# A decode-attention kernel without the GpSimd library: the identity and the maximum over partitions made by other engines

## The chip, the cores and the metric

The kernel runs on one core of one Trainium2 chip. The metric is the device time of one execution in microseconds (us); lower is better. The kernel before took 439.23 us, the median of its first three runs (438.93 to 439.62). One-core runs of one kernel agree within about 0.3%.

Names used below: PE is TensorE, PEld its weight loads, DVE VectorE, ACT ScalarE, POOL GpSimd, SP SyncE, which issues the loads. `L338` is line 338 of the kernel that the profile belongs to, so the same operation has another line in each kernel. "KB" in the lists of issues is 1024 bytes.

## The reference, cut to what matters

```python
def _A_ref(x, k_cache, v_cache, wq, wo):         # B=4, D=512, 32 query heads, 8 kv heads, Sk=8192, Dh=128
    q = (x @ wq) ...                             # one query token per batch
    scores = einsum("bhqd,bhkd->bhqk", q, k) * Dh ** -0.5
    p = softmax(scores, axis=-1)
    o = einsum("bhqk,bhkd->bhqd", p, v)
    return o @ wo
# _B_ref: the same with only the last W = 2048 positions of its cache
return concatenate([a, b], axis=-1)
```

Both caches are read once, in bf16. With the weights that is 184.56 MB, and almost no arithmetic per byte.

## The kernel before

The work is cut into 20 units, four for B and then 16 for A. Each unit has 4 MB of K and 4 MB of V. Two units make one turn of a hardware loop. A unit's K is transposed on PE in 16 steps, evicted by DVE and ACT in turn, and multiplied with the queries. Then the softmax follows: maximum along the free axis on DVE, maximum over the partitions on POOL, subtraction on DVE, exponential on ACT. PV, the product with V, runs on PE one unit later. The parts that the change touches:

```python
def pool_ar1(u):                                    # the maximum over partitions, a library operation
    n = ncol(u)
    def fn(pool):
        return pool.partition_all_reduce(MB[:, 0:n], M1m[:, 0:n], channels=128, reduce_op=ReduceOp.max)
    return dict(eng="pool", fn=fn, waits=[("pm", u, 0)], inc=("ar1", u))

def pool_setup0(pool):                              # all memsets first
    ...                                             # dummy, onesf, onesb, RQ, OT_sb, oacc, PT
    return pool.memset(Wo_sb[:, :, :], 0.0)
op("pool", pool_setup0, inc=("pset",))
def pool_setup1(pool):                              # then the identity, bf16 and fp32
    ins = pool.affine_select(out=ident[:, :], in_=onesb[:, :], pattern=[[1, 128]], compare_op=AluOpType.is_equal, ...)
    ins = pool.affine_select(out=identf[:, :], in_=onesf[:, :], ...)
    return ins
op("pool", pool_setup1, waits=[("pset",)], inc=("setup",))
...
# the order of PE in a unit: T0 T1 T2 (T3 S0) ... T15 S12, sums of u-1, S13, X, S14, S15, PV0 ... PV7 of u-1
# the order of DVE after the last scores:
add(dve_max(u, 1)); ...; add(dve_addmask(u))
add(dve_sum(u - 1)); add(dve_rcp(u - 1))            # beside the all-reduce
add(dve_submask(u)); add(dve_sub(u, 0)); add(dve_sub(u, 1)); add_norm(u - 1)
```

PE waits on absolute semaphore counts, so each turn ends by taking the turn's share off every semaphore that PE waits on:

```python
with nc.Fori(0, n_turn, engines=[engine]):
    run(turns[0])
    for n, sem in by_name.items():
        pe.sem_inc(sem, -strides[n])
```

The loads are issued by SP in one queue: Wq of B, Wq of A, K of unit 0, K of unit 1, then V and K of the following units as their two buffer slots come free, and at the end the last quarter of Wo in eight pieces (`Wl_sb`).

## Time and profile before

| what | number | how to read it |
|---|---|---|
| time, span of the profile | 439.23 us, 437.0 us | the span is the profiled execution |
| DMA, queue q1 | 99.1% of 16 engines | the loads fill the span |
| PE busy | 365.0 us, 84% | second |
| DVE, ACT, POOL busy | 48%, 45%, 6% | far from full |
| last weight piece lands | about 434.4 us | PE's last waits are for it |

The profile's other lines of before are shown in the prediction below. L888 is the line with the `sem_inc` above; "PEq" is PE's sequencer:

```profile
PE KT L283 <- PEq L888: 4.1, 3, 1.4
```

PE's first transposes of a turn stand up to 1.4 us behind those resets. In the trace's records of PE's sequencer the last loop end of before has 11 resets, from 425.08 to 426.59 us, 0.15 us apart.

### The profile page before, as it was taken

Reading aid. Unit: us, or ns where it says so; the run is one execution under the profiler, and the core shown is the slowest. Engines: PE = TensorE matmul, PEld = TensorE weight load, DVE = VectorE, ACT = ScalarE, POOL = GpSimd, SP = SyncE. Lnnn points to the kernel's source line nnn. Section 1 sums busy time; section 2 is a strip of 40 time slices with the busy share of each in tenths; the row PEclk is TensorE's granted clock in tenths of the full one; section 3 lists DMA queues with packets and bytes.
Section 4 is the critical chain, followed back from the end, with each engine's and each line's share of the span. In section 5 each row is a group of like instructions: output and inputs, shape, how many; then the busy total and the mean of one; then the engine's idle time right before and its main releaser. Section 6 shows DMA issues by size and latency. Waiting matters only on the chain.

```text
span 437.0 us, 15525 instructions
## 1 busy us (share of the span) xinstructions
PE 365.0 (84%) x7174; PEld 337.9 (77%) x7184; DVE 210.0 (48%) x406; ACT 195.0 (45%) x249; POOL 27.7 (6%) x88
## 2 busy tenths in 40 slices
PE   0168898998998959895989598969868996989996
PEld 0158897997997949795979588868868886979975
DVE  0004455664564634563456247525643563455651
ACT  1024473573653625371634254434534462536530
POOL 6100000000000000000000000000100000000000
PEclk9999999999999988999999899989996999799999
DMA  8999999999999999999999999999999999999996
GB/s 340 430 421 421 429 412 430 418 439 412 445 432 432 424 438 432 432 432 432 432 432 429 432 432 430 431 433 432 410 454 432 432 432 432 432 432 411 447 407 255
DMA packets 10996, 184.73 MB, mean 423 GB/s; under 512 B 1236, under 2 KB 2280, under 8 KB 2408
## 3 DMA queue, kind: packets, MB, share of 16 engines
q1 hardware_dynamic: 10960, 184.56, 99.1%
q8 instruction: 8, 0.13, 0.1%
q14 instruction: 4, 0.03, 0.0%
q10 hardware_dynamic: 24, 0.01, 0.0%
HBM read 184.56 MB, written 0.01 MB: 422 GB/s over the span
## 4 chain that ended last, share of the span: by engine, by line
PE 54%; DMA 40%; issue 2%; DVE 1%; SPq 1%; ACT 1%
DMA K_sb<-in_A_k_cache_dram 29%; PE KT L283 27%; PE OT L338 11%; DMA K_sb<-in_B_k_cache_dram 7%; PE SB L322 5%; PE SA L322 4%; DMA V_sb<-in_A_v_cache_dram 4%; PE KT L396 4%; PE SA L350 1%; PE KT L338 1%; SPq L566 1%; DVE oacc L404 1%; PE KT L263 1%; ACT KT_sb L299 1%; DVE OS L501 0%
## 5 line engine op out<-in xcount | busy, mean ns | idle before, releaser
L283 PE MATMUL KT<-identf,K_sb 128*128 128x128 f32 x1280 | 207.6, 296 | 44.1 <-DMA K_sb<-in_A_k_cache_dram 30.7
L299 ACT ACTIVATE KT_sb<-KT 128x1024 bf16<-128x1024 bf16 (+1 forms) x192 | 165.1, 881 | 120.6 <-PE KT L283 120.6
L283 PEld LDWEIGHTS KT<-identf,K_sb 128*128 128x128 f32 x1280 | 147.6, 150 | 49.3 <-DMA K_sb<-in_A_k_cache_dram 31.7
L299 DVE COPY KT_sb<-KT 128x512 int32<-128x512 int32 x160 | 110.5, 691 | 132.1 <-PE KT L283 130.7
L338 PE MATMUL OT<-PT,V_sb 128*128 128x64 bf16 x2560 | 78.1, 193 | 1.6 <-issue 1.1
L338 PEld LDWEIGHTS OT<-PT,V_sb 128*128 128x128 bf16 x2560 | 75.9, 98 | 1.8 <-issue 1.2
L469 ACT ACTIVATE PT<-Dt 128x512 bf16<-128x512 f32 x40 | 24.6, 630 | 84.0 <-DVE Dt L458 84.0
L322 PEld LDWEIGHTS SA<-RQc,KT_sb 128*128 128x128 bf16 x1280 | 56.9, 98 | 2.3
L322 PEld LDWEIGHTS SB<-RQc,KT_sb 128*128 128x128 bf16 x1280 | 51.1, 97 | 7.9 <-issue 4.4
L322 PE MATMUL SA<-RQc,KT_sb 128*128 128x16 bf16 x1280 | 56.4, 170 | 0.0
L322 PE MATMUL SB<-RQc,KT_sb 128*128 128x16 bf16 x1280 | 52.9, 170 | 0.0
L420 DVE TENSOR_REDUCE M<-SB 128x8 f32<-128x512 f32 (+1 forms) x20 | 13.8, 692 | 50.0 <-PE SB L322 50.0
L441 POOL PARTITION_ALL_REDUCE MB<-M1m x20 | 7.7, 387 | 334.3 <-DVE M1m L434 334.3
L396 PE MATMUL KT<-Wo_sb,OL 128*4 128x512 bf16 x80 | 18.9, 379 | 0.0
L201 PE MATMUL KT<-ident,x_sb 4*128 4x4 bf16 x8 | 0.6, 170 | 19.9 <-POOL identf L537 19.9
L201 PEld LDWEIGHTS KT<-ident,x_sb 4*128 4x128 bf16 x8 | 0.4, 112 | 20.1 <-issue 20.1
L476 DVE TENSOR_REDUCE LB<-SA 128x8 f32<-128x512 f32 (+1 forms) x20 | 13.7, 684 | 2.8 <-PE SA L350 2.8
L458 DVE TENSOR_TENSOR Dt<-SA,MBm 128x512 f32<-128x512 f32 x20 | 13.8, 692 | 0.7
L367 DVE TENSOR_TENSOR ORx<-KT,MSK 32x1024 bf16<-32x1024 bf16 x10 | 12.1, 1211 | 3.3 <-PE KT L362 3.3
L458 DVE TENSOR_TENSOR Dt<-SB,MBm 128x512 f32<-128x512 f32 x20 | 13.6, 681 | 0.0
L420 DVE TENSOR_REDUCE M<-SA 128x8 f32<-128x512 f32 (+1 forms) x20 | 13.6, 681 | 0.0
L350 PE MATMUL SA<-PT,onesb 128*128 128x128 bf16 x168 | 12.7, 218 | 0.0
(69 smaller groups left out, 118.0 us busy)
## 6 DMA issues: line engine op xcount, KB each, us to landing
K_sb<-in_A_k_cache_dram SPq DMA_DIRECT2D x15, 4096.0 KB, 22.5
V_sb<-in_A_v_cache_dram SPq DMA_DIRECT2D x15, 4096.0 KB, 30.3
K_sb<-in_B_k_cache_dram SPq DMA_DIRECT2D x8, 2048.0 KB, 23.6
V_sb<-in_B_v_cache_dram SPq DMA_DIRECT2D x16, 1024.0 KB, 18.4
V_sb<-in_B_wq_dram SPq DMA_DIRECT2D x1, 4096.0 KB, 12.5
V_sb<-in_A_wq_dram SPq DMA_DIRECT2D x1, 4096.0 KB, 21.8
Wo_sb<-in_B_wo_dram SPq DMA_DIRECT2D x4, 1024.0 KB, 11.9
K_sb<-in_A_k_cache_dram SPq DMA_DIRECT2D x2, 2048.0 KB, 17.5
```

Source lines behind the costliest of these rows:

```text
L283: ins = pe.transpose(out=bkf[:, pi * 128:(pi + 1) * 128], in_=K_sbf[:, slot, t0:t0 + 2, :].rearrange("p t d -> p (t d)"), identity=identf[ ...
L299: ins = e.tensor_copy(out=d, in_=r) if eng == "dve" else e.activation(out=d, in_=r, func=ACTF.Copy)
L322: ins = pe.matmul(out=stb[:, t % NTH * C:(t % NTH + 2) * C], lhsT=ktv[:, pi, :, e], rhs=RQc[:, u % 2, t // TS, e, :], start=(e == 0), stop ...
L338: ins = pe.matmul(out=otb[:, s * NW:s * NW + w], lhsT=V_sb[:, slot, t, :], rhs=PT[:, slot, t * C:t * C + w], start=(j == 0), stop=(j == n ...
L350: ins = pe.matmul(out=SA[u % 2][:, s * NM:(s + 1) * NM], lhsT=onesb[:, :], rhs=PT[:, u % 2, c0:c0 + NM], start=(i == 0), stop=(i == n - 1))
L367: return dve.tensor_tensor(out=ORx[:, :, :, :], in0=bk[0:NR, 0:128].rearrange("p (i o r) -> p r o i", o=1, r=C).broadcast_to([NR, C, C, 12 ...
L396: ins = pe.matmul(out=bk[0:Bn, 0:D], lhsT=OL[:, i, :], rhs=Wo_sb[:, i, :], start=(i == 0), stop=(i == C - 1))
L420: return dve.tensor_reduce(out=M1[:, h * n:(h + 1) * n].rearrange("p (s h) -> p s h", h=C), in_=bank[:, :].rearrange("p (s j h) -> p s h j ...
L441: return pool.partition_all_reduce(MB[:, 0:n], M1m[:, 0:n], channels=128, reduce_op=ReduceOp.max)
L458: return dve.tensor_tensor(out=Dt[:, h * NTH * C:(h + 1) * NTH * C].rearrange("p (s j h) -> p s j h", s=Sh, h=C), in0=bank[:, :].rearrange ...
L469: return act.activation(out=PT[:, u % 2, a:b], in_=Dt[:, a:b], func=ACTF.Exp, scale=scale)
L476: return dve.tensor_reduce(out=LB[:, 0:n].rearrange("p (s h) -> p s h", h=C), in_=SA[u % 2][:, 0:NSEG * NM].rearrange("p (s j h) -> p s h ...
```

## The change

The intent is to do without the GpSimd library, whose load was taken to hold up the start (the gap of 11.13 us in the prediction's lines). The identity comes from a running sum on VectorE, a 32x32 transpose and a comparison, copied to four diagonal blocks; the long memsets go behind it. The maximum over partitions becomes a PE transpose, a VectorE maximum, a diagonal matrix, and a PE product with ones that spreads it to all partitions. Core of the diff (cuts marked):

```diff
-                return pool.partition_all_reduce(MB[:, 0:n], M1m[:, 0:n], channels=128, reduce_op=ReduceOp.max)
+        def pe_MT(u):
+            op("pe", lambda pe: pe.transpose(out=mtx(u), in_=M1m[:, :], identity=identf[:, :]), waits=[("pm", u, 0)], inc=("mt", u))
+        def dve_mx(u):     # tensor_reduce max of mtx(u) into MX, waits mt
+        def dve_dg(u):     # DG = identf * MX (a diagonal), waits mx
+        def pe_MB(u):
+            op("pe", lambda pe: pe.matmul(out=mbx(u), lhsT=onesf[0:NX, :], rhs=DG[:, :], start=True, stop=True), waits=[("dg", u)], inc=("ar1", u))
...
-        def pool_setup1(pool):
-            ins = pool.affine_select(out=ident[:, :], ...
+        op("pool", lambda pool: pool.memset(ONE[:, :], 1.0), inc=("pl", 0))
+        op("dve", lambda dve: dve.tensor_tensor_scan(out=JC, data0=ONE, data1=ONE, initial=0.0, op0=mult, op1=add), ...)
+        op("dve", lambda dve: dve.transpose(out=JR, in_=JC), ...)
+        op("dve", lambda dve: dve.tensor_tensor(out=EQ, in0=JC, in1=JR, op=is_equal), ...)
+        def pool_identf(pool):    # EQ to the four diagonal 32x32 blocks of identf; ident is a copy of identf
...
+        op("pool", pool_setup, inc=("pset",))       # the memsets, now after the masks
...
+            if pc == 3: TOK.append(("MT",))         # PE: transpose after three PV chunks
+            if pc == 5: TOK.append(("MB",))         # PE: broadcast after five
...
+            if u >= 1:
+                add(dve_sum(u - 1))                 # the sum moves ahead of the second maximum
             add(dve_max(u, 1))
```

Left out of the cut: GpSimd's copies of the queries wait for a new signal from PE (`rqf`), and PE, DVE and ACT wait for the moved memsets (`pset`).

More of the change, by code (lines that the diff above doesn't have):

```diff
@@ L28, in bass_concat_heads__gqa_block_cached__sliding_block_cached__decode_kernel @@
 ):
-    ReduceOp = bass.bass_isa.ReduceOp
     Bn, _, D = A_x.shape
@@ L99, in bass_concat_heads__gqa_block_cached__sliding_block_cached__decode_kernel @@
         M1m = sb("M1m", [128, NSEG * C], F32)
-        MB = sb("MB", [128, NSEG * C], F32)
         MBm = sb("MBm", [128, NSEG * C], F32)
@@ L114, in bass_concat_heads__gqa_block_cached__sliding_block_cached__decode_kernel @@
         ORx = sb("ORx", [C * Bn, C, C, 128 // C], BF16)
+        ONE = sb("ONE", [128, 32], F32)
+        JC = sb("JC", [128, 32], F32)
+        JR = sb("JR", [128, 32], F32)
+        EQ = sb("EQ", [128, 32], F32)
+        MX = sb("MX", [NSEG * C, 1], F32)
+        DG = sb("DG", [NSEG * C, NSEG * C], F32)
         MSK = sb("MSK", [C * Bn, C], BF16)
@@ L128, in bass_concat_heads__gqa_block_cached__sliding_block_cached__decode_kernel @@
                  "out0", "out1", "out2", "Tq", "Td", "Ta", "S", "PV", "Ed", "Ea", "Eq", "vs", "sub", "exp", "otr", "otp",
-                 "ocp", "Ef", "fin0", "fin1", "ar1", "SM", "msk", "pset", "setup", "pm0", "pm1", "oc", "ocB", "mkb", "perm", "rq"]
+                 "ocp", "Ef", "fin0", "fin1", "ar1", "mt", "rqf", "dg", "jj", "pl", "SM", "msk", "pset", "setup", "pm0", "pm1", "oc", "ocB", "mkb", "perm", "rq"]
         sems = {n: sm("s_" + n) for n in names}
@@ L159, in sem_of @@
                 return sems["Ed"] if jobs[key[1]]["eng"] == "dve" else sems["Ea"]
-            return sems["vs" if t in ("max", "maxc", "sum", "rcp", "os") else t]
+            return sems["vs" if t in ("max", "maxc", "sum", "rcp", "os", "mx") else t]
         DMA_KEYS = ("K", "Kh", "KH", "V", "Vh", "VL", "WL", "x", "out", "WQ", "wo")
@@ L253, in efn @@
                 return ins
-            add(dict(eng="act", fn=efn, waits=[("T", idx)], inc=("E", idx)))
+            add(dict(eng="act", fn=efn, waits=[("T", idx), ("pset",)], inc=("E", idx)))
         def pe_filler(n):
@@ L304, in pool_rq @@
             un = units[u]
-            w = [("E", perm_idx[un["P"]])]
+            w = [("E", perm_idx[un["P"]])] + ([("rqf", u - 2)] if u >= 2 else [])
             if un["P"] == 1:
@@ L340, in fn @@
                 return ins
-            op("pe", fn, waits=waits, inc=("PV", u * NC + c))
+            op("pe", fn, waits=waits, inc=("rqf", u + 1) if c == 0 and bank is None else ("PV", u * NC + c))
         def pe_SM(u):
@@ L435, in dve_addmask, with mtx, mbx @@
             return dict(eng="dve", fn=fn, waits=[("max", u, 1) if P == 1 else ("maxc", u)] + ([("mkb",)] if u == 0 else []), inc=("pm", u, 0))
-        def pool_ar1(u):
-            n = ncol(u)
-            def fn(pool):
-                return pool.partition_all_reduce(MB[:, 0:n], M1m[:, 0:n], channels=128, reduce_op=ReduceOp.max)
-            return dict(eng="pool", fn=fn, waits=[("pm", u, 0)], inc=("ar1", u))
+        NX = NSEG * C
+        def mtx(u):
+            return SA[(u + 1) % 2][0:NX, 0:128]
+        def mbx(u):
+            return SA[(u + 1) % 2][:, 128:128 + NX]
+        def pe_MT(u):
+            op("pe", lambda pe: pe.transpose(out=mtx(u), in_=M1m[:, :], identity=identf[:, :]), waits=[("pm", u, 0)], inc=("mt", u))
+        def dve_mx(u):
+            n = ncol(u)
+            return dict(eng="dve", fn=lambda dve: dve.tensor_reduce(out=MX[0:n, :], in_=mtx(u)[0:n, :], axis=AX.X, op=AluOpType.max),
+                        waits=[("mt", u)], inc=("mx", u))
+        def dve_dg(u):
+            n = ncol(u)
+            return dict(eng="dve", fn=lambda dve: dve.tensor_scalar(out=DG[0:n, :], in0=identf[0:n, 0:NX], scalar1=MX[0:n, :], scalar2=None,
+                                                                    op0=AluOpType.mult), waits=[("mx", u)], inc=("dg", u))
+        def pe_MB(u):
+            op("pe", lambda pe: pe.matmul(out=mbx(u), lhsT=onesf[0:NX, :], rhs=DG[:, :], start=True, stop=True), waits=[("dg", u)], inc=("ar1", u))
         def dve_submask(u):
@@ L447, in fn @@
             def fn(dve):
-                return dve.tensor_tensor(out=MBm[:, 0:n], in0=MB[:, 0:n], in1=MASK[P][:, 0:n], op=AluOpType.subtract)
+                return dve.tensor_tensor(out=MBm[:, 0:n], in0=mbx(u)[:, 0:n], in1=MASK[P][:, 0:n], op=AluOpType.subtract)
             return dict(eng="dve", fn=fn, waits=[("ar1", u)], inc=("pm", u, 1))
@@ L520, in pool_otp, with pool_first @@
             return dict(eng="pool", fn=lambda pool: pool.tensor_copy(out=OTp[:, :, :], in_=OT_sb[:, P, q, :, :]), waits=w, inc=("otp", tn))
-        def pool_setup0(pool):
+        def pool_first(pool):
+            pool.memset(identf[:, :], 0.0)
             pool.memset(dummy[:, :], 0.0)
             pool.memset(onesf[:, :], 1.0)
-            pool.memset(onesb[:, :], 1.0)
-            pool.memset(RQ[0][:, :, :, :, :], 0.0)
-            pool.memset(RQ[1][:, :, :, :, :], 0.0)
-            pool.memset(OT_sb[:, :, :, :, :], 0.0)
-            pool.memset(oacc[:, :], 0.0)
-            pool.memset(PT[:, :, :], 0.0)
-            return pool.memset(Wo_sb[:, :, :], 0.0)
-        op("pool", pool_setup0, inc=("pset",))
-        def pool_setup1(pool):
-            ins = pool.affine_select(out=ident[:, :], in_=onesb[:, :], pattern=[[1, 128]],
-                                     compare_op=AluOpType.is_equal, fill=0.0, base=0, channel_multiplier=-1)
-            ins = pool.affine_select(out=identf[:, :], in_=onesf[:, :], pattern=[[1, 128]],
-                                     compare_op=AluOpType.is_equal, fill=0.0, base=0, channel_multiplier=-1)
-            return ins
-        op("pool", pool_setup1, waits=[("pset",)], inc=("setup",))
+            return pool.memset(onesb[:, :], 1.0)
+        op("pool", lambda pool: pool.memset(ONE[:, :], 1.0), inc=("pl", 0))
+        op("pool", pool_first, inc=("pl", 1))
+        op("dve", lambda dve: dve.tensor_tensor_scan(out=JC[:, :], data0=ONE[:, :], data1=ONE[:, :], initial=0.0, op0=AluOpType.mult,
+                                                     op1=AluOpType.add), waits=[("pl", 0)], inc=("jj", 0))
+        op("dve", lambda dve: dve.transpose(out=JR[:, :], in_=JC[:, :]), waits=[("jj", 0)], inc=("jj", 1))
+        op("dve", lambda dve: dve.tensor_tensor(out=EQ[:, :], in0=JC[:, :], in1=JR[:, :], op=AluOpType.is_equal), waits=[("jj", 1)], inc=("jj", 2))
+        def pool_identf(pool):
+            ins = None
+            for q in range(4):
+                ins = pool.tensor_copy(out=identf[32 * q:32 * q + 32, 32 * q:32 * q + 32], in_=EQ[32 * q:32 * q + 32, :])
+            return ins
+        op("pool", pool_identf, waits=[("jj", 2), ("pl", 1)], inc=("pl", 2))
+        op("pool", lambda pool: pool.tensor_copy(out=ident[:, :], in_=identf[:, :]), waits=[("pl", 2)], inc=("setup",))
         def pool_perm(pool):
@@ L562, in bass_concat_heads__gqa_block_cached__sliding_block_cached__decode_kernel, with pool_setup @@
         op("pool", pool_mask2, waits=[("msk",)], inc=("mkb",))
+        def pool_setup(pool):
+            pool.memset(RQ[1][:, :, :, :, :], 0.0)
+            pool.memset(RQ[0][:, :, :, :, :], 0.0)
+            pool.memset(OT_sb[:, :, :, :, :], 0.0)
+            pool.memset(oacc[:, :], 0.0)
+            pool.memset(PT[:, :, :], 0.0)
+            return pool.memset(Wo_sb[:, :, :], 0.0)
+        op("pool", pool_setup, inc=("pset",))
         def dma(dst, src):
@@ L579, in bass_concat_heads__gqa_block_cached__sliding_block_cached__decode_kernel @@
             pe_job_perm(P)
-        op("pe", None, waits=[("E", perm_idx[0]), ("setup",), ("msk",)])
-        op("dve", None, waits=[("msk",)])
+        op("pe", None, waits=[("E", perm_idx[0]), ("setup",), ("msk",), ("pset",)])
+        op("dve", None, waits=[("msk",), ("pset",)])
         add(pool_rq(0))
@@ L598, in bass_concat_heads__gqa_block_cached__sliding_block_cached__decode_kernel @@
             pc += 1
+            if pc == 3:
+                TOK.append(("MT",))
+            if pc == 5:
+                TOK.append(("MB",))
         assert pc == NC
@@ L624, in bass_concat_heads__gqa_block_cached__sliding_block_cached__decode_kernel @@
                     pe_SM(u - 1)
+                elif tok[0] == "MT":
+                    pe_MT(u)
+                elif tok[0] == "MB":
+                    pe_MB(u)
                 else:
@@ L643, in bass_concat_heads__gqa_block_cached__sliding_block_cached__decode_kernel @@
             if u >= 1:
-                add(dve_sum(u - 1))
                 add(dve_rcp(u - 1))
+            add(dve_mx(u))
+            add(dve_dg(u))
             add(dve_submask(u))
@@ L667, in bass_concat_heads__gqa_block_cached__sliding_block_cached__decode_kernel @@
                 add(pool_rq(u + 1))
-            add(pool_ar1(u))
             if u >= 1 and units[u - 1]["P"] == 0:
```

## The prediction

> **What bounds the kernel now.** I read the page from the top: busy shares, the tenths by slice, the DMA queue table.
>
> ```profile
> span 437.0 us, 15525 instructions
> DMA  8999999999999999999999999999999999999996
> GB/s 340 430 421 421 429 412 430 418 439 412 445 432 432 424 438 432 432 432 432 432 432 429 432 432 430 431 433 432 410 454 432 432 432 432 432 432 411 447 407 255
> q1 hardware_dynamic: 10960, 184.56, 99.1%
> ```
>
> The 16 DMA engines are full in every slice but the first and the last, and move 432 GB/s in most. 184.56 MB at 432 GB/s is 427.2 us, which leaves 9.8 us of the 437.0 us span for the start, a slightly slower first third, and the tail. PE, at 84% busy, is second. The question for this change is therefore not what an engine saves, but whether the DMA queue starts earlier, runs dry, or is followed by a longer tail.
>
> Second, the windows view over stretches I chose. Columns: window, length, busy time of PE, PEld, DVE, ACT, POOL with counts, PE clock, DMA share, GB/s.
>
> ```profile
> 8.00:19.20 11.20, 0.00 (x0) 0.00 (x0) 0.00 (x0) 0.00 (x0) 0.12 (x1) 1.00 0.99 424
> 34.00:90.00 56.00, 53.24 (x1027) 50.03 (x1030) 30.77 (x54) 29.82 (x55) 2.24 (x7) 1.00 1.01 422
> 141.00:270.00 129.00, 109.21 (x2066) 101.55 (x2070) 65.15 (x126) 58.49 (x62) 5.92 (x24) 0.95 1.00 431
> ```
>
> From 8 to 19 us every compute engine is idle while DMA runs at 99%. From 34 to 90 us PE is nearly full as well (53.24 of 56): it is catching up. From 141 us on it has 15% to spare.
>
> Third, the chain that ended last, in order of time (start, length, what):
>
> ```profile
> 2.38 31.46 DMA K_sb<-in_B_k_cache_dram
> 33.88 3.68 PE KT L283 x16
> ...
> 408.76 17.94 DMA V_sb<-in_A_v_cache_dram
> ```
>
> The first cache block lands at 33.84 us because it stands behind two 4 MB Wq loads in one queue. Nothing on the compute side touches that. The last V load is waited for too.
>
> Fourth, the timeline of the start (start, length, engine, line, operation) with the queue's issues:
>
> ```profile
> 4.62 3.51 POOL L531 MEMSET Wo_sb<- 128x4096 bf16 x1
> 19.26 0.28 POOL L535 TENSOR_SCALAR_AFFINE_SELECT ident<-onesb 128x128 bf16<-128x128 bf16 x1 [11.13 <-issue]
> 24.15 2.94 SPq L566 DMA_DIRECT2D V_sb<-in_B_v_cache_dram  x4
> ```
>
> The memsets end at 8.13 us, then GpSimd stands 11.13 us before the first select: the library load that the change removes. The identity exists at 19.8 us, the first V loads are issued at 24.15 us.
>
> Fifth, the timeline of one unit's end (unit 18), where the reduction sits:
>
> ```profile
> 404.41 3.89 PE L338 MATMUL OT<-PT,V_sb 128*128 128x64 bf16 x128
> ...
> 405.51 0.17 DVE L434 TENSOR_TENSOR M1m<-M1c,MASKA 128x8 f32<-128x8 f32 x1
> 405.60 0.68 DVE L476 TENSOR_REDUCE LB<-SA 128x8 f32<-128x512 f32 x1
> 405.78 0.37 POOL L441 PARTITION_ALL_REDUCE MB<-M1m  x1 [13.96 <-DVE M1m L434]
> 406.32 0.20 DVE L483 RECIPROCAL RL<-LB 128x8 f32<-128x8 f32 x1
> 406.44 0.11 DVE L448 TENSOR_TENSOR MBm<-MB,MASKA 128x8 f32<-128x8 f32 x1
> ...
> 407.19 0.68 DVE L458 TENSOR_TENSOR Dt<-SB,MBm 128x512 f32<-128x512 f32 x1
> ```
>
> The all-reduce takes 0.37 us and hides wholly behind VectorE's sum and reciprocal: VectorE goes from one to the next without a gap. It is not slow once loaded.
>
> **What the Trainium skill says.** "DMA: Bandwidth & Descriptors", section "Where 436 GB/s comes from", gives 435.2 GB/s as the fabric ceiling, but says that for HBM to SBUF about 358 binds. The trace has 431 GB/s for 129 us, so here the fabric ceiling is the one that fits, and there is no rate left to win. "GPSIMD Engine Reference", section "When to use GPSIMD", lists the cross-partition reduce as GpSimd's alone; in the trace it costs 387 ns on average; I found no page with the 11 us load. "VectorE: DVE Perf Modes", section "The TRN2 errata", gives (N+151)/0.96 ns for an fp32 two-input operation: 691 for 512 elements against 692 in the trace, and 166 for 8 elements against 167. I use it for the new small operations. "TensorE: Matmul & The Clock Gate", section "PE-mode transpose", gives about 275 ns in a kernel for a 128x128 bf16 transpose; the trace's fp32 ones on L283 take 296 ns each and four of them advance PE by 0.49 us.
>
> **The change part by part.** (1) Start. Removed: 11.13 us of library load and the 8 us of memsets ahead of the identity, which move behind it. Added: some ten small operations on VectorE and GpSimd at 0.1 to 0.3 us (rows of that size take that), with a few hand-overs: the identity should be there at about 3 us instead of 19.8. The moved memsets are then done at about 11 us. But the first Q projection needs Wq for B, whose load was issued at 0.80 us and lands at about 13.3 us (12.5 us median landing in the table of DMA issues), so it starts at about 13.5 us instead of 20.5, and the first V loads are issued at about 17 us instead of 24.15. At 24.15 us the queue had 16 MiB (16.8 MB) issued and, by the GB/s row, 9.4 MB moved: 17 us of work. An earlier issue only lengthens it. Worth on the end: 0 us. Wq for A lands at about 23 us and K at 33.84 us as before, so PE starts the caches at the same 33.9 us.
>
> (2) Per unit, 20 times. GpSimd loses 0.37 us, nobody's bound. The sum moves ahead of the second maximum, into VectorE's 1.87 us wait for the last scores: free. PE gets an fp32 transpose after three of the eight PV chunks and an fp32 matmul after five. A chunk is 3.75/8 = 0.47 us, so PE reaches the transpose at 404.41 + 1.41 = 405.82 us, and the masked maxima are ready at 405.68: no wait, or a tenth. The transpose costs PE about 0.15 to 0.2 us of issue; its result is there at about 406.15. Maximum over 128: (128+151)/0.96 = 0.29 us; diagonal: 0.17 us; ready at about 406.7. PE comes to the broadcast at 405.82 + 0.2 + 0.94 = 406.96, so again does not wait; an fp32 product is two passes in this trace (L679), say 0.3 us of issue, result at about 407.3. The subtraction of the mask starts there instead of at 406.44: 0.9 us later. Both subtractions end at about 408.8 (before 407.87). PE's last chunk ends 0.2 + 0.3 = 0.5 us later, so the norm and the next unit's first eviction shift by 0.5 us. Sum: 0.5 us per unit on PE and VectorE, 10 us in all, of which the question is how much shows.
>
> (3) Does the queue run dry? Taking issued megabytes from the list of issues and moved ones from the GB/s row: at 54.77 us 25.2 MB issued and 22.4 moved, 2.8 MB or 6.5 us in hand; at 123.99 us 54.5 and 51.9, 6.1 us in hand; at 183.97 us 80.7 and 77.8, 6.9 us in hand. Up to 124 us PE never waits for K, so delays add up: five units, 2.5 us, against 6.1. After that each pair of units starts with a K landing (30.7 us of such waits, in 8 turns), which forgives the delay of the pair before: 1 us against 6.9. The queue stays full: 0 us.
>
> (4) Tail. The last wait for K before the end is at 370.7 us; four units follow, 2.0 us of delay, of which the 0.5 us wait for V at 421.85 and the 1.3 us wait at 427.08 take 1.8.
>
> ```profile
> 427.08 1.98 PE L338 MATMUL KT<-PT,V_sb 128*128 128x64 bf16 x64 [1.33 <-DMA V_sb<-in_A_v_cache_dram]
> ...
> 434.47 0.08 PEld L700 LDWEIGHTS KT<-Wl_sb,OT_sb 128*4 128x4 bf16 x1 [0.23 <-DMA Wl_sb<-in_A_wo_dram]
> ```
>
> What is left, 0.2 us, meets a 0.46 us wait for V at 430.4 and small waits for Wl. Worth 0 to 0.3 us. Sum: 439.23 + 0 + 0 + 0.1 = 439.3 us.
>
> **Rivals.** (a) The start is on the path and its 11 to 17 us are won: about 425 us. For it: PE sat 19.9 us before its first instruction, its longest single wait. Against: the DMA share of 0.99 in those microseconds, and a floor of 427.2 us at this rate before any tail. (b) PE meets VectorE in order and stalls twice a unit, 1 us or more each: 20 units by 2 us or more empty the 6 us cushion before 124 us, and the tail grows: 442 to 455 us. For it: PE at 53.24 of 56 us and my slacks of 0.14 and 0.26 us are thin. Against: one missed slack costs tenths, not a microsecond. (c) The library load takes memory traffic that the packet table does not list: 0.3 to 0.7 us won. The rate of 424 while it loads, against 431 later, leaves room for 0.2 us at most; a start at 394 from 2 to 8 us is before it. (d) Each unit's delay is 1 us instead of 0.5: the tail gets 1 to 2 us, 440 to 441 us.
>
> **Range and chances.** The three runs before span 0.7 us; (c) pulls down by half a microsecond, (d) up by one. 438.5 to 440.4 us. Faster by 2% needs 430.4 us, below what this queue can do with its tail: 0.01. Slower by 2% needs (b) in full: 0.02. Within 2%: 0.97.
>
> **What would show it.** Right: span near 437; identity before 5 us, no long GpSimd gap; first Q products at about 13.5 us; V issued near 17 us; DMA share still 9s; K waited for until 33.8 us; MBm about 0.9 us later after the last scores than before; PE's PV stretch longer by about 0.5 us. Wrong: idle DMA slices after the first, the last K block landing later than before, PE waiting for VectorE inside PV by more than 0.3 us a unit, or a tail after the last Wl landing longer than the 2.6 us it has now.

## The result

The changed kernel took 439.87 us, the median of 6 runs (439.59 to 440.62), against 439.23 us for 6 runs of before (438.93 to 439.63). A ratio here is the mean time of one kernel's fast runs over that of the other's of the same rounds, so it is not quite the ratio of these medians: 1.0016, 95% interval 1.0003 to 1.0028. The kernel is the same within 2%, and 0.64 us slower by the medians, inside the predicted range of 438.5 to 440.4.

The page after, the lines that answer to those of before:

```profile
span 438.2 us, 15698 instructions
DMA  8999999999999999999999999999999999999995
GB/s 336 431 431 423 426 417 430 417 452 402 454 431 431 431 431 431 429 428 434 434 431 431 431 431 425 440 429 431 415 446 431 431 431 431 431 434 413 446 410 205
q1 hardware_dynamic: 10960, 184.56, 98.8%
```

The queue is as full as before, at the same rate; only the last slice has fallen, from 255 to 205 GB/s, because the span is longer behind the last loads. The windows view of the stretches shown for before, columns as there:

```profile
8.00:19.20 11.20, 4.19 (x134) 3.83 (x134) 0.00 (x0) 1.73 (x7) 4.09 (x4) 1.00 0.97 420
34.00:90.00 56.00, 53.77 (x1033) 50.37 (x1036) 32.19 (x60) 29.56 (x54) 1.04 (x4) 1.00 1.01 422
141.00:270.00 129.00, 113.15 (x2118) 104.73 (x2121) 70.33 (x143) 58.72 (x64) 3.76 (x18) 0.95 1.01 432
```

PE now works in the first window, and DMA moved no more for it (420 GB/s against 424). From 141 to 270 us PE has 113.15 us of work where it had 109.21, and DMA moves 432 instead of 431: PE's extra work costs nothing there.

The timeline of the start:

```profile
2.66 0.29 POOL L561 CAST ident<-identf 128x128 bf16<-128x128 f32 x1
13.05 3.58 PE L228 MATMUL KT<-xT,V_sb 128*128 128x4 bf16 x128 [9.70 <-DMA V_sb<-in_B_wq_dram]
16.66 3.12 SPq L596 DMA_DIRECT2D V_sb<-in_B_v_cache_dram  x4
33.83 2.40 PE L287 MATMUL KT<-identf,K_sb 128*128 128x128 f32 x10 [5.54 <-DMA K_sb<-in_B_k_cache_dram]
```

The identity is there at 2.95 us instead of 19.8, the first queries are projected when their weights land, the first V loads are issued 7.5 us earlier, and then PE waits 5.54 us for the same K block, which lands when it did before. The gain has become a wait.

The timeline of the end of unit 18, which was shown for before:

```profile
404.74 1.56 PE L342 MATMUL OT<-PT,V_sb 128*128 128x64 bf16 x48
...
405.85 0.17 DVE L438 TENSOR_TENSOR M1m<-M1c,MASKA 128x8 f32<-128x8 f32 x1
405.93 0.20 DVE L504 RECIPROCAL RL<-LB 128x8 f32<-128x8 f32 x1
406.11 0.10 PEld L450 LDWEIGHTS SA<-identf,M1m 128*32 128x32 f32 x1
...
406.44 0.28 DVE L454 TENSOR_REDUCE MX<-SA 8x1 f32<-8x128 f32 x1 [0.32 <-PE SA L450]
406.76 0.23 DVE L459 TENSOR_SCALAR DG<-identf,MX 8x32 f32<-8x32 f32 x1
407.27 0.40 PE L463 MATMUL SA<-DG,onesf 32*128 32x32 f32 x2
407.61 1.57 PE L342 MATMUL OT<-PT,V_sb 128*128 128x64 bf16 x48
407.71 0.17 DVE L469 TENSOR_TENSOR MBm<-SA,MASKA 128x8 f32<-128x8 f32 x1 [0.73 <-PE SA L463]
```

From PV's start to MBm is 407.71 - 404.74 = 2.97 us; before it was 406.44 - 404.41 = 2.03. PV with the two insertions lasts 407.61 + 1.57 - 404.74 = 4.44 us; before 3.89. So a unit costs PE 0.55 us more and the subtraction comes 0.94 us later. Neither insertion made PE wait.

The tail, where the last unit's PV begins:

```profile
428.37 1.98 PE L342 MATMUL KT<-PT,V_sb 128*128 128x64 bf16 x64 [1.66 <-ACT PT L490]
```

It stood at 427.08 after a gap of 1.33 us; now it stands at 428.37 after a gap of 1.66. The end follows: SP's last store is issued at 436.44 us instead of 435.33.

**Where the 1.1 us of the profiled run come from.** The two profiled runs took 438.96 and 439.96 us, so they lie further apart than the medians. The trace's records of PE's sequencer show 13 resets at the last loop end instead of 11, from 426.04 to 427.89 us: 0.15 us apart, 0.3 us more. The PV just ahead of it, in unit 19, waits for V. Before, from the table of waits; after, from the timeline:

```profile
PE OT L338 <- DMA V_sb<-in_A_v_cache_dram: 0.5, 1, 0.5
422.26 1.57 PE L342 MATMUL OT<-PT,V_sb 128*128 128x64 bf16 x48
```

V lands at 421.80 us before and at 422.21 after, and each time this PV starts 0.05 us later. So what PE lost before this point, in units 17 and 18 or at the loop end between them, has no effect behind it. Three parts make up the 1.29 us: V landed 0.41 us later, this PV lasts 0.55 longer, and the loop end behind it takes 0.33 more. The last steps give back 0.18, because before, PE waited 0.18 and 0.23 us for the last weight pieces, and now it does not. The 0.41 us go back to one slow load near 190 us, of which the run "changed, again" says more. Of the 1.29 us only 0.88 belong to the change.

**A difference of clock that hides ahead of this wait.** Unit 18 starts only 0.33 us later than before (391.98 against 391.65), which looks like one loop end, but is not. After PE's wait for K near 371 us the trace grants half clock until 376.41 us before, and only until 374.67 after (the windows view from 371 to 376 us has 0.50 and 0.66). PE gets that K 0.41 us later, needs 0.96 us less from there to unit 17's PV, then 0.55 more for the insertion and 0.33 more for the loop end. From that K to unit 18, start_only below, with 3.4 us at half clock like the changed kernel, takes 20.01 us, and the changed kernel 20.85: with like clocks the difference is 0.84, close to 0.55 + 0.33. The wait for V then takes that up.

### The profile page after: what moved, and what is told of

The parts are those of the page before. It is cut to its first block, busy times and chain, and to the rows that moved or that the text cites. A ratio compares the mean times of both kernels' runs of the same rounds, so it can differ in the third digit from the quotient of the medians.

```text
span 438.2 us, 15698 instructions
## 1 busy us (share of the span) xinstructions
PE 373.1 (85%) x7234; PEld 344.4 (79%) x7244; DVE 223.1 (51%) x449; ACT 194.9 (44%) x249; POOL 21.0 (5%) x73
## 4 chain that ended last, share of the span: by engine, by line
PE 52%; DMA 36%; PEld 4%; DVE 3%; issue 2%; SPq 1%; ACT 1%; PEldq 0%
DMA K_sb<-in_A_k_cache_dram 28%; PE KT L287 25%; PE OT L342 9%; DMA K_sb<-in_B_k_cache_dram 7%; PE SB L326 5%; PE SA L326 4%; PE KT L400 4%; DVE Dt L479 2%; PEld KT L287 2%; PE SA L354 1%; PE SA L463 1%; PE KT L342 1%; SPq L596 1%; DVE oacc L408 1%; PEld OT L342 1%
## 5 line engine op out<-in xcount | busy, mean ns | idle before, releaser
L287 PE MATMUL KT<-identf,K_sb 128*128 128x128 f32 x1280 | 204.8, 293 | 40.0 <-DMA K_sb<-in_A_k_cache_dram 20.9
L287 PEld LDWEIGHTS KT<-identf,K_sb 128*128 128x128 f32 x1280 | 144.9, 148 | 45.0 <-DMA K_sb<-in_A_k_cache_dram 21.7
L342 PE MATMUL OT<-PT,V_sb 128*128 128x64 bf16 x2560 | 83.7, 193 | 0.2 <-issue 0.2
L342 PEld LDWEIGHTS OT<-PT,V_sb 128*128 128x128 bf16 x2560 | 79.0, 98 | 1.5 <-issue 0.3
L228 PE MATMUL KT<-xT,V_sb 128*128 128x4 bf16 x256 | 7.1, 166 | 16.2 <-DMA V_sb<-in_B_wq_dram 9.7
L228 PEld LDWEIGHTS KT<-xT,V_sb 128*128 128x128 bf16 x256 | 7.0, 104 | 16.4 <-DMA V_sb<-in_B_wq_dram 9.8
L531 POOL COPY OT_sb<-ON 128x8 bf16<-128x8 bf16 x15 | 3.0, 203 | 294.7 <-DVE ON L525 294.7
```

The lines of the kernel that those rows point to most:

```text
L228: ins = pe.matmul(out=bk[:, hl * Bn:(hl + 1) * Bn], lhsT=wv[:, c, hq * DH:(hq + 1) * DH], rhs=xT[:, P, c, :], start=(c == 0), stop=(c == D ...
L287: ins = pe.transpose(out=bkf[:, pi * 128:(pi + 1) * 128], in_=K_sbf[:, slot, t0:t0 + 2, :].rearrange("p t d -> p (t d)"), identity=identf[ ...
L342: ins = pe.matmul(out=otb[:, s * NW:s * NW + w], lhsT=V_sb[:, slot, t, :], rhs=PT[:, slot, t * C:t * C + w], start=(j == 0), stop=(j == n ...
```

## The experiments

Every kernel here gave correct results. Ratios are against the kernel before in the same rounds.

| kernel | median us (runs) | ratio, 95% interval | V for unit 19's PV lands at | last PV starts at |
|---|---|---|---|---|
| before | 439.25 (9) | 1 | 421.80 | 427.08 |
| changed | 439.87 (6) | 1.0016, 1.0003 to 1.0028 | 422.21 | 428.37 |
| start_only | 439.28 (5) | 1.0002, 0.9989 to 1.0016 | 421.95 | 427.27 |
| reduce_only | 440.07 (5) | 1.0020, 1.0006 to 1.0034 | 422.00 | 428.55 |
| fewer_resets | 439.42 (5) | 1.0009, 0.9995 to 1.0023 | 421.79 | 427.63 |
| late_identity | 440.66 (5) | 1.0036, 1.0022 to 1.0050 | 422.90 | 429.07 |
| one_pass | 439.68 (5) | 1.0008, 0.9994 to 1.0022 | 422.23 | 428.17 |
| one_pass_fewer | 439.31 (5) | 1.0002, 0.9989 to 1.0016 | 421.85 | 427.47 |
| pe_dose_half | 439.66 (5) | 1.0010, 0.9997 to 1.0024 | 422.11 | 427.94 |
| pe_dose_two | 446.53 (5) | 1.0172, 1.0158 to 1.0185 | 426.61 | 434.87 |
| resets_dose | 443.80 (6, one slow; 443.34 of the five fast) | 1.0096, 1.0065 to 1.0127 | 422.42 | 429.24 |
| changed, again | 439.64 (6) | 1.0011, 0.9999 to 1.0024 | 421.99 | 428.12 |

The last two columns give one sum for all of these kernels. The last PV starts later than before by the later landing of V, plus what unit 19's PV has gained in length (0.55 us with the full insertion, 0.33 with the one-pass one), plus what the loop end has gained (0.33 with 13 resets). For "changed, again" that is 0.19 + 0.55 + 0.30 = 1.04. Only in reduce_only and pe_dose_two does PE reach this PV after V, 0.40 and 0.88 us late, and that comes on top; in reduce_only the trace grants half clock until 375.88 us.

### One half of the change at a time

start_only takes the changed kernel and puts the all-reduce back:

```diff
-            op("pe", ... transpose ...); dve_mx; dve_dg; op("pe", ... matmul ones x DG ...)
+            return pool.partition_all_reduce(MB[:, 0:n], M1m[:, 0:n], channels=128, reduce_op=ReduceOp.max)
```

> The kernel before with the new start alone: identity from the VectorE scan, the memsets behind it, the library's all-reduce kept (its own library is then loaded between about 19 and 49 us, as before between 26.5 and 49 us, while GpSimd is idle). My theory (DMA sets the end, the start is hidden behind the 33.8 us landing of the first K block): within 0.3 us of the kernel before, identity at about 3 us. Rival (the start is worth its microseconds and the new reduction took them back): 5 to 15 us faster.

The time is that of before (1.0002). Its timeline on GpSimd shows something else:

```profile
2.64 0.29 POOL L546 CAST ident<-identf 128x128 bf16<-128x128 f32 x1
14.86 0.19 POOL L564 TENSOR_SCALAR MASKA<-EO 128x8 f32<-128x8 f32 x1 [11.11 <-issue]
```

The identity is early, but the 11.11 us gap is still there, now ahead of the masks, where the changed kernel has no gap. Nothing waits for it. So the start alone is worth nothing (interval 0.9989 to 1.0016), and the rival that it was worth 5 to 15 us, eaten up again by the reduction, is refuted.

reduce_only keeps the new maximum and puts the memsets first and the select-built identity behind them:

```diff
+            ins = pool.affine_select(out=ident[:, :], in_=onesb[:, :], ... fill=0.0, base=0, channel_multiplier=-1)
-        op("dve", lambda dve: dve.tensor_tensor_scan(...)) ...
```

> The changed kernel with the old start: select-built identity behind the 11.1 us library load, the new maximum over partitions kept. My theory (the 0.64 us comes from the reduction's cost on PE in the last two units and at two loop ends): 0.5 to 1.1 us slower than the kernel before, the same as the changed kernel within 0.3 us, PV of the last unit starting about 1.3 us later than before (427.08). Rival (the moved memsets or the earlier V loads disturb the DMA stream and cost the 0.64 us): as the kernel before.

It is as slow as the changed kernel (1.0020 against 1.0016), and the last PV starts at 428.55 us after the same 1.66 us gap. The whole loss comes with the reduction. One thing in what I had expected was wrong: there was no library load.

```profile
4.63 3.51 POOL L552 MEMSET Wo_sb<- 128x4096 bf16 x1
8.21 0.29 POOL L556 TENSOR_SCALAR_AFFINE_SELECT ident<-onesb 128x128 bf16<-128x128 bf16 x1
```

The select follows the last memset at once; in the kernel before the same select stood 11.13 us. The gap comes with the all-reduce being in the program (before, start_only), and not with the select. It stands where GpSimd first changes its configuration: the trace's records of GpSimd's sequencer have MODIFY_POOL_CONFIG at 8.15 us in before and at 3.78 in start_only, just ahead of the gap. reduce_only and the changed kernel have that record too, at 8.09 and 3.73 us, without a gap. A second one stands ahead of the first all-reduce (26.54 in before, 24.19 in start_only, where I had expected 19); what follows it can't be seen, since GpSimd has nothing to do there. By which mechanism the gap arises, no run here shows.

### Is the start really hidden?

late_identity delays the changed kernel's identity by about 21 us with memsets ahead of it:

```diff
+        for i in range(4):
+            op("pool", lambda pool: pool.memset(Wo_sb[:, :, :], 0.0), waits=[...], inc=("lag", i))
         op("pool", lambda pool: pool.memset(ONE[:, :], 1.0), inc=("pl", 0))
```

> The changed kernel with all memsets and four more of 3.5 us ahead of the identity, which then comes at about 24 us instead of 2.9. My theory (hidden until the first K block lands at 33.8 us): the changed kernel's time within 0.3 us, first V loads issued at about 27 us. Rival (start on the path): 15 to 20 us slower.

It came to 440.66 us, 0.8 us over the changed kernel (which ran in other rounds; by the two ratios it is 0.9): far from 15 to 20 us, but not within 0.3. The reason is in the trace. The second projection ended late, so PE began the caches at 36.3 instead of 33.8 us. That delay lived on while PE was catching up: the K load that the changed kernel issues at 125.69 us was issued at 130.04, with less still in hand. Counted as bytes issued less the bytes of completed packets, at 432 GB/s, there were 1.5 us instead of 5.5 (7.7 in before at the same load). The windows view of the ten microseconds after it:

```profile
130.00:140.00 10.00, 10.00 (x173) 9.85 (x172) 6.13 (x9) 7.79 (x9) 0.00 (x0) 1.00 0.98 393
```

393 GB/s, where the changed kernel has 439 in that window. The queue was not empty, but thin, and from the next load on the landings are about 1 us later than in the changed kernel. So 21 us of delay at the start cost 0.8 us, through the cushion.

### Which part of the reduction costs?

fewer_resets counts the two new signals on the semaphore of VectorE's evictions, on which PE waits anyhow:

```diff
+            if t == "dg" or (t == "pm" and key[2] == 0):
+                return sems["Ed"]
             if t == "pm":
```

> The changed kernel with the two signals that PE newly waits for counted on the semaphore of VectorE's evictions, so that PE's loop ends with 11 semaphore resets again instead of 13. Each reset takes 0.15 us of PE's sequencer in the trace. My theory: the gap at PE's loop end goes from 1.66 back to about 1.35 us, twice on the path of the tail (before unit 18 and before the last PV): 0.3 to 0.6 us faster than the changed kernel. Rival (the exit is hidden behind DMA or exp): no change against the changed kernel.

```profile
427.63 1.56 PE L344 MATMUL KT<-PT,V_sb 128*128 128x64 bf16 x48 [1.33 <-ACT PT L492]
```

The gap at the loop end is 1.33 us again. The median is 439.42, 0.45 us below the changed kernel's, as expected, though the intervals of the two ratios overlap; what shows the mechanism is the gap, the size rests on it and on one_pass_fewer below. My theory had the loop end twice on the path. It is there once: V lands as before (421.79 us), and the last PV starts 0.55 us later than before, which is one insertion. The loop end ahead of unit 18 stands before the wait for V.

one_pass makes the broadcast one pass by keeping the diagonal in bf16. All partitions still subtract the same number, so the softmax stays exact up to rounding:

```diff
-        DG = sb("DG", [NSEG * C, NSEG * C], F32)
+        DG = sb("DG", [NSEG * C, NSEG * C], BF16)
-            ... lhsT=onesf[0:NX, :], rhs=DG[:, :]
+            ... lhsT=onesb[0:NX, :], rhs=DG[:, :]
```

> The changed kernel with the diagonal and the ones in bf16, so that the broadcast is one pass on PE instead of two (the maximum is rounded, but the same value is subtracted on every partition, so the softmax stays right). My theory: PE's step at the broadcast goes from about 0.34 to about 0.2 us, three units of it in the tail: 0.2 to 0.5 us faster than the changed kernel, 439.4 to 439.7 us. Rival (VectorE's longer chain alone counts, not PE's time): no more than 0.1 us.

It took 439.68 us: 0.2 us less than the changed kernel, at the upper end of what I expected and within the noise of this comparison. I had counted three units of the shorter product; unit 19's PV is 0.22 us shorter (4.24 instead of 4.46), once. Its gap before the last PV is still 1.66 us. one_pass_fewer has both repairs.

> Both repairs together on the changed kernel: one-pass broadcast and the two signals counted on the evictions' semaphore. My theory: PE reaches the last PV within 0.3 us of the kernel before, so the last weight landing sets the end again: 439.1 to 439.4 us, the same as before within 0.2 us, and not faster, since DMA and its tail bound both. Rival: it stays 0.3 us or more behind, because VectorE's later subtraction of the maximum is on the path.

```profile
303.68 0.18 PE L465 MATMUL SA<-DG,onesb 32*128 32x32 bf16 x1
```

The product lasts 0.18 us instead of 0.40. The time is 439.31 us, 1.0002 of before. All five runs (439.17 to 439.59) lie at or below the fastest run of the changed kernel. VectorE's longer chain is still there in this kernel and costs nothing visible. It does not beat before. But the reason that I had given, the last weight landing, is not what the trace shows: that piece lands at 434.5 us as before, and PE runs through its last products from 433.15 to 435.06 us without a wait for any of them, 0.2 us behind before (434.85), which did wait.

### Doses on the kernel before

pe_dose_half and pe_dose_two leave the maximum alone and add only PE time, 5 or 19 unused products per unit:

```diff
+                if c == 4 and bank is None:
+                    for _ in range(5):              # 19 in pe_dose_two
+                        pe.matmul(out=OTB[:, NSEG * NW:512], lhsT=ident[:, :], rhs=permE..., start=True, stop=True)
```

> The kernel before with nothing but PE time added: five unused products of 256 columns, about 0.55 us, in the middle of each unit's PV. No change to the maximum, VectorE or semaphores. My theory (PE time in the last three units is what the change costs): 0.4 to 0.9 us slower than before, not 20 x 0.55 = 11 us. Rival (the cost is VectorE's later chain or the extra semaphores alone): within 0.2 us of before.

It took 439.66 us, half a microsecond over before, with the last PV at 427.94 and the gap unchanged at 1.33 us: PE time by itself gives what the change's PE time gives: V landed 0.31 us later, and the PV lasts 0.54 longer. (The interval of the ratio includes 1; the size rests on this trace.) 20 units times 0.55 us would have been 11.

> The same with 19 products, about 2 us a unit. Tests the cushion of queued DMA. My theory: at about 124 us five units' delay, 10 us, meets 7.7 us of queued loads, the queue runs dry by 2 to 3 us and every later landing is 2.5 to 4 us late; later turns lose nothing more; the tail adds three units less half a microsecond: 5 us. Sum 7 to 9 us slower, 446 to 448.5 us. Rival A (the queue never matters, only the tail): about 5 us slower. Rival B (PE time is on the path in every unit): 40 us slower.

It took 446.53 us, 7.4 us slower, within what I had expected. The windows view:

```profile
130.00:140.00 10.00, 10.00 (x188) 9.76 (x185) 4.78 (x9) 5.90 (x7) 0.00 (x0) 1.00 0.60 242
```

DMA worked 60% of these ten microseconds (100% in before): the K load that before issues at 123.99 us was issued at 133.79, after the queue had run out. The landings are 4.1 us later from there and 4.9 at the end; the other 2.5 us are the tail. So the sum was right partly by luck: I had put the dry queue at 2.5 to 4 us and the tail at 5, and the two errors cancel. Part of the shorter tail is the clock: PE's last wait for K is only 2.15 us long here, and the trace grants the full clock after it, so that PE takes 20.41 us from that K to unit 18, 0.40 more than start_only for 2.06 more work. Neither rival fits, neither 5 us without any loss of DMA nor 40.

resets_dose splits the resets at PE's loop end in two on the kernel before:

```diff
-                    pe.sem_inc(sem, -strides[n])
+                    if name == "pe" and strides[n] >= 2:
+                        pe.sem_inc(sem, -1)
+                        pe.sem_inc(sem, 1 - strides[n])
+                    else:
+                        pe.sem_inc(sem, -strides[n])
```

> The kernel before with nothing changed but PE's loop end: each semaphore's reset that takes 2 or more is done in two instructions, 8 to 10 more in all, at 0.15 us each 1.2 to 1.5 us more per loop end. My theory (the loop end is on PE's path before unit 18 and before the last PV, and only waits for V give some back): the last PV starts 1.5 to 2.5 us later, the end 1.2 to 2.2 us later, 440.4 to 441.4 us; no change to the landings. Rival (the 1.33 us before the last PV is a wait for V, as my prediction read it, and hides a longer loop end): within 0.3 us of before.

```profile
429.24 0.96 PE L338 MATMUL KT<-PT,V_sb 128*128 128x64 bf16 x25 [2.87 <-issue]
```

Ten resets more took the gap from 1.33 to 2.87 us, 0.154 us each, and the last PV starts 2.16 us later, within what I had expected. Of this, 0.62 us is a later landing of V, though I had expected the landings unchanged. V had landed at 427.3, so the gap hides nothing: the rival falls. The time is a miss on the high side, 443.8 us with runs from 441.06 to 448.04, one of them counted as slow. The window right after the gap shows why:

```profile
428.00:432.00 4.00, 2.76 (x66) 2.79 (x67) 0.00 (x0) 0.00 (x0) 0.00 (x0) 0.74 0.97 378
```

The granted PE clock is 0.74 there and was 1.00 in before. After this longer idle time the trace grants half speed for 3.4 us, and the same 64 products take 2.83 us instead of 1.98. The same happens at other loop ends of this run (near 110, 270 and 392 us, for instance), and its times follow the clock: 441.06 us at a mean granted clock of 0.961, 445.17 at 0.946. So this run confirms where the gap stands, and its total is not a measure of resets alone.

> The changed kernel once more, on the same chip and in the same rounds as the reset dose, to have its difference to the kernel before a second time: 0.5 to 0.8 us slower than before, and its last PV starting 1.0 to 1.4 us later than 427.08; the one 4 MB load that took 10.2 instead of 9.7 us near 190 us in its first profile should not come back there if that was chance.

The second set of runs of the changed kernel gave 439.64 us (1.0011), 0.49 us over before, with the last PV at 428.12. The slow 4 MB load near 190 us, 10.2 us in the first profile of the changed kernel, took 9.9 there and is taken for chance; it had moved the landings after it by 0.5 us. That is where V's later landing in the first profile comes from.

## Why the prediction was right

- **DMA sets the end, no rate to win.** Right: the rate, the landing of the first K block (33.84 and 33.79 us) and the full slices are unchanged.
- **(1) Start, worth 0.** Right, and shown by start_only. The times within it were right to half a microsecond (identity at 3, projection at 13.5, V issue at 17). Wrong was a reading that did not enter the sum: I put the library load down to the select, and reduce_only shows the select without a load.
- **(2) Per unit 0.5 us on PE, the subtraction 0.9 us later, no waits of PE.** Right: 0.55 and 0.94 us, and the transpose and the broadcast found their inputs ready.
- **(3) The queue stays full.** Right: at the load issued at 125.69 us, counted as in the prediction, 54.5 MB were issued and 52.8 moved, 3.9 us in hand, where the prediction had 6.1 less 2.5. The doses show where it ends: a delay of 6 us at this load (late_identity) lost 1 us of DMA, and one of 10 us lost 4.
- **(4) Tail, 0 to 0.3 us, taken as 0.1.** This is the mis-sized term: 0.64 us by the medians, 1.1 us in the profiled run. The step that failed is "the 0.5 us wait for V at 421.85 and the 1.3 us wait at 427.08 take 1.8" of the delay. The first was a wait for V and took up all that stood ahead of it: in the changed kernel, too, the PV starts 0.05 us after V's landing. The second was no wait for V, though the profile names V there: V had landed at 426.7, and PE's sequencer was still in its loop end, with the last reset at 426.59 and the branch until 426.92. A loop end moves along with what stands before it, so it takes up nothing. It even grew, by two resets of 0.15 us for the two semaphores that PE newly waits for, a cost that the prediction's list of parts had not got. So one insertion and one longer loop end, 0.88 us, stand behind the wait for V; less the 0.18 given back at the end that is 0.7, near the 0.64 and 0.49 us of the medians. The 0.46 us at 430.4, "a wait for V" in the prediction, took up next to nothing either: in the changed kernel PE starts there 0.91 us after V has landed and has still stood 0.43 us. I had also counted four units behind the last K wait; unit 17 is the first of three. That the time fell inside the range is owed to the width left for rival (d), not to this sum.
- **Rivals.** (a), the start is won, is refuted by start_only and late_identity. (b), PE stalls in order, did not occur, though pe_dose_two shows that its threshold was rightly placed: 2 us a unit make 7.4 us. (c), traffic of the library load, is not seen: 424 GB/s with it, 420 without. (d), a unit's delay of 1 us, was not the size of the unit's delay, but it named the right place, the tail.

## What to carry to other kernels

Where one queue of loads is full from start to end, ask of a change only three things: does the first load start earlier, does the queue ever run low, and what stands behind the last load. Work out the cushion (bytes issued less bytes moved) at each issue: anything that delays an issue by less is free, and anything that speeds up a start ahead of it gains nothing. A wait for a load wipes out what was lost before it: count only what stands behind the last one. In the tail, look at what the sequencer does in a gap before you count the gap as slack: a wait takes up a delay, but a loop end only passes it on (1.33 us here, whether PE came early or late), and each further semaphore that the loop must reset makes it longer (0.15 us here). Compare the clock of the two profiles in each stretch before you put a difference down to the change.

## What the Trainium skill lacked or had wrong

- "GPSIMD Engine Reference", section "Instruction dispatch", which the prediction did not find, gives approximately 6 us for the first call to a freshly loaded kernel. Here 11.1 us stand on GpSimd at its first change of configuration in the kernels with the all-reduce, and none in those without it, whether they use the select or not. Whether this is that load is not shown. The page also says, in the section "When to use GPSIMD", that the cross-partition reduce is GpSimd's only; here TensorE and VectorE do it at 0.55 us of PE time a unit, and with a one-pass broadcast and shared semaphores at the same total time (1.0002).
- "DMA: Bandwidth & Descriptors", section "Where 436 GB/s comes from", has about 358 GB/s binding for HBM to SBUF; one core read at 431 GB/s for 129 us. The same passage calls its own measurement at 16 MB, 425 GB/s, near the fabric's rate: this run, on one core alone, sides with that.
- No page that I found has the cost of a semaphore reset on PE's sequencer in a loop: 0.15 us each here, in line, 1.33 us of gap with 11 and 1.66 with 13.
- "TensorE: Matmul & The Clock Gate", section "What's actually happening", puts the drop to half clock after an idle window of about 3.4 us. In these traces the window need not be wholly idle. I laid consecutive windows of 3.41 us, counted from the first clock record, through each of the 12 traces up to 430 us. All 64 drops follow a window with 1.89 us or more of PE idle (as the profile models it), and none of the other 1221 windows at full clock had more than 1.85. The clock came back after windows with 0.67 us idle or less, and stayed at half with 0.71 or more. So the gap of 2.87 us in resets_dose was followed by half clock for 3.4 us, and gaps of 1.33 and 1.66 us at the same place were not.
- No page has how thin a queue may get: with about 1.5 us of loads in hand at an issue (by completed packets), the rate over ten microseconds was 393 GB/s; with 5.5 us in hand it was 439.
